# A delta-rule attention and two MLPs in one kernel: another written-out order for the first layer, and the last output tile shared by two engines

## The chip, the cores and the metric

One core of one Trainium2 chip runs the whole program. The metric is the device time of one execution in microseconds (us), as the median of several runs. A profile is one more execution, recorded by the hardware profiler; times inside it count from its first instruction.

## What is computed

Three stages follow each other, all in fp32 on the outside:

```python
# attention, per batch and head, over 768 steps t (head_dim 48)
k_n = k / (norm(k) + 1e-6)
y[t]  = q[t] @ state
state = state + beta[t] * outer(k_n[t], v[t] - state.T @ k_n[t])
# first layer: 3072 tokens, 384 -> 2048 -> 384
h = maximum(x @ w_in, 0); x = (h * h) @ w_out
# second layer: 3072 tokens, 384 -> 1536 -> 384
out = (sigmoid(x @ w_gate) * (x @ w_val)) @ w_out2
```

The weights come in as 64-bit words that hold doubles; the kernel turns them into fp32 itself.

## The kernel before, in words

**Precision.** A product with the weights is made of three: each operand is kept as a high and a low part (`xhi`, `xlo`; `w1h` and what is loaded as `il`; `gh`, `gl`), and hi*hi, lo*hi and hi*lo are added up in PSUM. The attention's products are plain fp32, and the trace shows each of them as two matmuls.

**Attention.** The 768 steps are cut in chunks of 64; two chunks (`st` 0 and 1) form a group `g`, 0 to 5. For each chunk small matmuls (16 to 64 rows and columns) make the scores (`scores_a`, L346; `scores_p`, L364), the inverse of a triangular matrix (rows on VectorE, `row16` L439 and `row` L448; the joins L483 to L521 for group 0 and 1; `n_piece` L523, `w_piece` L538), what the old state gives (`ks_piece`, L550), the new rows (`t_piece`, L571), the new state (`s_piece`, L582) and the output (`y_piece`, L600). Chunk after chunk hangs on the state of the one before. `y_rows` (L619) moves an output by DMA from `yt` to `xr`, where features lie along partitions; in group 0 three of its seven DMAs are issued by ScalarE, all others by SyncE. `x_split` (L638) makes `xhi` on ScalarE and `xlo` on VectorE.

**First layer.** `moe1_h` (L677) makes one of 16 blocks of 128 hidden units for the 512 tokens of a group: 9 matmuls of 128x512, then three passes on ScalarE (`relu2`, L681). `moe1_g` (L692) makes `gl` on VectorE, `moe1_o` (L701) adds the block to the output with 9 more matmuls. Numbers run through: `h,17` is group 1, block 1. The low parts of the weights are read back from DRAM into rings of three buffers each (`fetch_low`, L648).

**Conversion of the first layer's weights.** For each block f: fetch (`f`), two ScalarE passes (`hi`, L151), a shift on VectorE (`b`, L157), an addition on VectorE (`b2`, L160), the high part on ScalarE (`ch`, `parts` L201), the low part on GpSimd (`cl`, `rests` L207), and its store (`sl`, `keep` L211). The three steps `hi`, `b`, `b2` stand in both programs alike. The second layer's weights go through the same (`w2,i,k`).

**What sets the order.** `ORDER` (L41) is a list of 921 tokens such as `h,17` or `ks,0,1` (names in the table `fns`, L747; a token's numbers are group and chunk, or block). The loop at L766 runs them one after the other, and every engine and DMA queue executes what it gets strictly in that order, waiting by semaphores for what others make. `d,n` are n spare matmuls. The list ends with `h,80` and `h,81`; the rest of the first layer (L942) and the whole second layer are emitted by loops with plans of their own.

**The end.** The last group's output is made in four tiles `m` of 36 matmuls each (L1169 to L1191). Tile 0 and 2 are copied out of PSUM by ScalarE, 1 and 3 by VectorE; SyncE stores each in two DMAs.

Of the kernel before, what the change touches and what calls it, by code (L numbers as in the profile page):

```python
# [46 lines left out]
b2,5 a,1,1 ti,1 sl,3 y,0,0 r,1,0 s,0,0 r,1,1 cl,4 f,6 f,7 r,1,2 sl,4 z,0,0 hi,6 ks,0,1 d,1 b,6 b2,6 d,1 ch,5
cl,5 x,0,0 kc,1,1 t,0,1 hi,7 y,0,1 r,1,3 r,1,4 d,1 d,2 to,1 b,7 p,1,1 f,8 sl,5 q,1,0 v,1,0 z,0,1 b2,7 ch,6 cl,6
x,0,1 ja,1,1 hi,8 p,1,0 h,0 ja,1,0 ch,7 kn,2,0 b,8 li,2 h,2 t1,1 g,0 li,1 b2,8 h,1 sl,6 g,2 li,3 lw,3 g,1 sv,1,0
cl,7 lw,0 ch,8 o,0 f,9 lw,2 s,0,1 hi,9 b,9 sl,7 jb,1,1 f,10 h,3 b2,9 ks,1,0 lw,1 kt,2,1 cl,8 n,1,1 hi,10 g,3  # L50
sq,2,0 sl,8 b,10 ch,9 li,7 sm,3,0 o,1 cl,9 jb,1,0 f,11 b2,10 h,7 sm,2,0 o,2 hi,11 b,11 b2,11 jc,1,0 li,4 kn,2,1
sl,9 ch,10 sq,2,1 lw,4 n,1,0 sm,2,1 jc,1,1 no,2 h,4 cl,10 f,12 hi,12 a,2,1 g,4 ch,11 li,5 o,3 b,12 sl,10 g,7 h,5
lw,5 a,2,0 b2,12 w,1,0 o,4 cl,11 f,13 hi,13 b,13 g,5 li,6 lw,6 b2,13 li,8 w,1,1 lw,7 ti,2 t,1,0 k2,1,0 h,6 y,1,0
r,2,0 v,1,1 o,5 g,6 ch,12 s,1,0 sl,11 kz,2,0 r,2,1 h,8 f,14 sv,1,1 ks,1,1 li,9 o,6 cl,12 sl,12 li,10 hi,14 b,14
ch,13 cl,13 g,8 b2,14 li,11 lw,8 o,7 h,9 g,9 r,2,2 r,2,3 t,1,1 z,1,0 x,1,0 h,11 o,8 lw,9 h,10 sl,13 ch,14 f,15
hi,15 g,11 b,15 g,10 b2,15 y,1,1 o,9 li,12 h,12 g,12 lw,11 p,2,0 li,13 lw,10 r,2,4 r,2,5 cl,14 lw,12 o,10 ch,15
sl,14 z,1,1 li,14 h,13 x,1,1 o,11 g,13 h,14 g,14 lw,13 li,16 o,12 h,16 r,2,6 lw,14 cl,15 sl,15 k2,1,1 v,2,0 o,13
o,14 li,15 h,15 r,2,7 li,18 g,16 lw,15 g,15 h,18 s,1,1 kz,2,1 o,15 g,18 r,2,8 li,17 h,17 g,17 lw,16 li,21 r,2,9
lw,18 sv,2,0 o,16 li,19 kn,3,1 h,19 lw,17 r,2,10 to,2 o,17 g,19 w2,0,0 o,18 t1,2 sq,3,1 h,21 li,20 sm,3,1 w2,0,1
p,2,1 lw,20 no,3 n,2,0 lw,19 o,19 h,20 q,2,0 kc,2,0 ks,2,0 w,2,0 g,20 lw,25 kt,3,1 w2,0,2 v,2,1 li,24 h,24 n,2,1  # L60
a,3,1 g,24 o,20 sv,2,1 w2,0,3 q,2,1 g,21 kt,3,0 li,23 a,3,0 li,22 h,22 g,22 w,2,1 ti,3 r,3,0 li,25 t,2,0 lw,21
o,21 k2,2,0 r,3,1 r,3,2 lw,22 o,22 po,0 h,23 g,23 ks,0,0 lw,23 y,2,0 h,25 o,23 r,3,3 r,3,4 li,26 h,26 kc,2,1
li,28 g,25 lw,24 o,24 kz,3,0 s,2,0 z,2,0 x,2,0 r,3,5 o,25 li,27 h,27 g,26 g,27 k2,2,1 lw,26 ks,2,1 v,3,1 kn,4,1
h,28 li,29 g,28 r,3,6 o,26 h,29 lw,27 t,2,1 o,27 li,31 w2,1,0 w2,1,1 y,2,1 li,30 r,3,7 h,30 lw,29 kn,5,0 sq,5,0
sq,4,1 g,29 r,3,8 lw,28 o,28 p,3,0 sm,4,1 h,31 w2,0,4 lw,30 li,32 li,34 z,2,1 lw,33 li,33 r,3,9 x,2,1 o,29 g,30
s,2,1 w2,1,2 h,32 o,30 g,31 h,34 w2,1,3 r,3,10 g,32 to,3 lw,31 o,31 kz,3,1 v,3,0 sv,3,0 h,33 p,3,1 g,33 kn,4,0
t1,3 n,3,0 li,35 lw,32 o,32 kc,3,0 g,34 sq,4,0 sm,4,0 no,4 o,33 li,37 w2,1,4 ks,3,0 li,36 n,3,1 kt,4,0 h,35
w2,2,0 w2,2,1 lw,34 h,36 w,3,0 g,35 a,4,0 o,34 lw,37 w2,2,2 li,38 kt,4,1 g,36 a,4,1 w,3,1 ti,4 lw,35 r,4,0 h,37
li,40 o,35 lw,36 h,40 po,1 g,37 r,4,1 r,4,2 o,36 t,3,0 r,4,3 o,37 r,4,4 h,38 kz,4,0 li,41 sv,3,1 g,38 q,3,0
w2,2,3 y,3,0 li,39 h,39 lw,38 o,38 lw,40 g,39 p,4,0 kc,3,1 g,40 r,4,5 li,43 lw,39 o,39 k2,3,0 s,3,0 r,4,6 h,43  # L70
z,3,0 h,41 o,40 g,41 ks,3,1 x,3,0 g,43 v,4,0 kc,4,0 li,42 li,44 lw,41 h,42 g,42 r,4,7 li,46 o,41 r,4,8 w2,2,4
t,3,1 r,4,9 r,4,10 q,3,1 h,44 y,3,1 w2,3,0 lw,42 o,42 g,44 li,45 w2,3,1 w2,3,2 lw,43 w2,3,3 o,43 kz,4,1 h,45
z,3,1 lw,44 p,4,1 g,45 x,3,1 li,47 h,46 o,44 lw,45 h,47 g,47 o,45 li,48 lw,52 li,49 lw,46 h,49 g,46 k2,3,1
w2,3,4 to,4 t1,4 lw,47 o,46 w2,4,0 h,48 g,49 w2,4,1 g,48 s,3,1 li,50 w2,4,2 li,52 n,4,0 sv,4,0 o,47 kn,5,1
w2,4,3 h,52 g,52 n,4,1 ks,4,0 kt,5,0 lw,48 o,48 sq,5,1 sm,5,1 sm,5,0 no,5 li,53 lw,49 h,50 w,4,1 li,51 kt,5,1
a,5,1 lw,50 v,4,1 o,49 w2,4,4 w2,5,0 sv,4,1 lw,51 h,51 w,4,0 w2,5,1 g,50 a,5,0 g,51 li,55 o,50 ti,5 h,53 w2,5,2
w2,5,3 o,51 q,4,0 t,4,0 lw,53 r,5,0 r,5,1 g,53 li,54 h,54 o,52 po,2 r,5,2 r,5,3 h,55 g,54 g,55 o,53 lw,54 y,4,0
w2,5,4 w2,6,0 w2,6,1 o,54 li,56 h,56 r,5,4 k2,4,0 w2,6,2 w2,6,3 li,57 lw,56 g,56 lw,55 s,4,0 h,57 g,57 kc,4,1
o,55 o,56 li,58 r,5,5 q,4,1 ks,4,1 lw,57 li,59 h,58 z,4,0 o,57 r,5,6 g,58 t,4,1 r,5,7 li,60 h,60 li,61 x,4,0
w2,6,4 lw,58 h,59 w2,7,0 g,59 o,58 lw,59 g,60 lw,60 li,62 lw,61 y,4,1 w2,7,1 k2,4,1 o,59 z,4,1 w2,7,2 w2,7,3  # L80
li,63 h,61 x,4,1 g,61 h,62 li,67 g,62 li,64 r,5,8 r,5,9 lw,62 o,60 h,63 lw,63 o,61 r,5,10 w2,8,0 h,64 li,66 g,64
g,63 s,4,1 to,5 w2,8,1 o,62 li,65 h,65 v,5,0 o,63 lw,66 w2,7,4 h,66 g,65 g,66 t1,5 lw,64 o,64 li,68 h,67 k2,5,0
g,67 w2,8,2 lw,65 q,5,0 kc,5,0 lw,68 w2,8,3 sv,5,0 o,65 o,66 h,68 lw,67 ks,5,0 n,5,0 li,69 kz,5,0 li,72 w2,9,0
h,69 g,68 o,67 w2,9,1 o,68 p,5,0 w,5,0 li,70 h,70 g,69 lw,69 w2,8,4 g,70 lw,70 h,72 lw,71 w2,9,2 o,69 li,71
li,74 w2,9,3 po,3 t,5,0 h,71 g,71 o,70 n,5,1 y,5,0 li,73 h,73 g,73 lw,72 w2,9,4 g,72 o,71 w2,10,0 lw,73 w2,10,1
li,76 w2,10,2 h,74 o,72 v,5,1 sv,5,1 o,73 g,74 li,77 h,76 g,76 w,5,1 s,5,0 li,75 h,75 z,5,0 lw,75 g,75 lw,74
# [1189 lines left out]
```

## Time and profile before

| | us |
|---|---|
| three timed runs | 1047.8, 1048.55, 1052.04 |
| median | 1048.55 |
| the profiled execution, its own time | 1056.13 |
| its span, first to last instruction | 1054.4 |
| TensorE busy in the span | 990.7 (94%) |
| mean granted TensorE clock | 0.991 |
| VectorE, ScalarE, GpSimd busy | 665.0, 502.6, 170.7 |
| DMA queue "instruction", q8 | 91 packets, 1.49 MB |

PE is TensorE's matmuls, PEld its weight loads, DVE VectorE, ACT ScalarE, POOL GpSimd, SP SyncE. A wait named "issue" is one in which the engine waited for nothing that the profile shows. A row of the timeline gives start, duration, engine, line, operation, out<-in, shape and count, and in brackets the idle time just before with what ended it.

### The profile page before, as it was taken

The numbers are of one execution on the slowest core, as the hardware profiler recorded it, in microseconds if no ns is written. First come the engines' busy times: TensorE is split into PE (matmuls) and PEld (weight loads), VectorE is DVE, ScalarE is ACT, GpSimd is POOL, SyncE is SP. The second block draws the span as 40 slices with busy tenths as digits, with TensorE's granted clock in tenths as the row PEclk, the third lists the DMA queues.
The fourth block names the chain that finished last, engine by engine and source line by source line (L and its number), as shares of the span: only waits on it lengthen the run. The fifth ranks groups of instructions, "written<-read, shape, count | busy, mean of one in ns | idle before, by whom it ended". The sixth has DMA issues, their size and how long they took to land. (4 is left out here: it accounts for less than half of the span.)

```text
span 1054.4 us, 27329 instructions
## 1 busy us (share of the span) xinstructions
PE 990.7 (94%) x11609; PEld 819.3 (78%) x11611; DVE 665.0 (63%) x1338; ACT 502.6 (48%) x827; POOL 170.7 (16%) x141
## 2 busy tenths in 40 slices
...
GB/s 259 204 167 165 215 219 189 207 200 129 203 211 194 192 202 216 179 189 203 175 188 215 239 227 235 234 259 128 213 173 140 104 127 97 91 134 165 121 2 59
DMA packets 84394, 186.31 MB, mean 177 GB/s; under 512 B 22320, under 2 KB 57520, under 8 KB 79664
## 3 DMA queue, kind: packets, MB, share of 16 engines
...
q8 instruction: 91, 1.49, 0.6%
...
HBM read 139.30 MB, written 40.50 MB: 171 GB/s over the span
## 5 line engine op out<-in xcount | busy, mean ns | idle before, releaser
L695 DVE TENSOR_TENSOR gl<-gg,gh 128x512 fp32r<-128x512 f32 x96 | 65.6, 688 | 106.5 <-ACT gg L689 106.4
L686 ACT ACTIVATE gg<-h 128x512 f32<-128x512 f32 x96 | 57.4, 598 | 143.7 <-PE h L672 140.6
L710 PE MATMUL o<-gh,il 128*128 128x512 f32 x288 | 113.8, 395 | 0.0
L997 PE MATMUL o<-gh,wo 128*128 128x512 f32 x270 | 91.7, 390 | 0.0
L710 PE MATMUL o<-gh,w1h 128*128 128x512 f32 x216 | 88.0, 407 | 0.0
L710 PE MATMUL o<-gl,w1h 128*128 128x512 f32 x216 | 85.7, 397 | 0.3 <-DVE gl L695 0.3
L672 PE MATMUL h<-xhi,il 128*128 128x512 f32 x288 | 82.0, 393 | 1.1 <-DMA il<-w1d 1.1
L1116 PE MATMUL gy<-xa,wg 128*128 128x512 f32 x288 | 75.5, 391 | 2.2 <-DVE gateC L1030 1.9
L1116 PE MATMUL gx<-xa,wg 128*128 128x512 f32 x288 | 75.5, 391 | 0.0
L303 POOL TENSOR_TENSOR v<-v,br 128x768 f32<-128x768 f32 x12 | 19.5, 1631 | 314.1 <-DMA v<-in_vn_dram 193.0
L1116 PEld LDWEIGHTS gy<-xa,wg 128*128 128x128 f32 x288 | 53.8, 188 | 14.6 <-DVE gateC L1030 3.0
L672 PE MATMUL h<-xhi,w1h 128*128 128x512 f32 x216 | 64.4, 407 | 0.4 <-ACT xhi L126 0.4
L672 PEld LDWEIGHTS h<-xhi,il 128*128 128x128 f32 x288 | 54.5, 189 | 13.2 <-DMA il<-w1d 1.5
L1116 PEld LDWEIGHTS gx<-xa,wg 128*128 128x128 f32 x288 | 53.9, 188 | 12.3 <-DVE valC L1030 0.7
L710 PEld LDWEIGHTS o<-gh,il 128*128 128x128 f32 x288 | 54.9, 191 | 10.7
L688 ACT ACTIVATE gh<-gg 128x512 fp32r<-128x512 f32 x96 | 60.7, 632 | 3.1
L689 ACT ACTIVATE gg<-gg 128x512 f32<-128x512 f32 x96 | 60.7, 632 | 3.1
L672 PE MATMUL h<-xlo,w1h 128*128 128x512 f32 x216 | 61.2, 392 | 0.0
L997 PEld LDWEIGHTS o<-gh,wo 128*128 128x128 f32 x270 | 50.7, 188 | 10.6
L997 PE MATMUL o<-gl,wo 128*128 128x512 f32 x135 | 52.6, 390 | 0.0
L462 DVE TENSOR_TENSOR tt<-tt,tmp 128x40 f32<-128x40 f32 (+7 forms) x208 | 49.2, 269 | 1.4
L850 POOL TENSOR_TENSOR wg<-wr,wg 128x640 fp32r<-128x640 f32 (+1 forms) x20 | 30.9, 1552 | 116.1 <-ACT wg L845 116.1
(221 smaller groups left out, 2173.6 us busy)
## 6 DMA issues: line engine op xcount, KB each, us to landing
...
```

Source lines behind the costliest of these rows:

```text
L303: nc.gpsimd.tensor_tensor(out=v, in0=v, in1=br[:, 16 * st:16 * st + 16].unsqueeze(2).to_broadcast([128, 16, HD]), op=ALU.mult)
L462: nc.vector.tensor_tensor(out=tt[:, 0:j, lo:hi], in0=tt[:, 0:j, lo:hi], in1=tv[i], op=ALU.subtract)
L672: nc.tensor.matmul(out=ps[:, cs], lhsT=w[:, kc * 128:kc * 128 + 128], rhs=x[:, kc, cs], start=(i == 0 and kc == 0), stop=(i == 2 and kc == ...
L686: nc.scalar.activation(out=gg, in_=ps, func=ACTF.Relu)
L688: nc.scalar.activation(out=gh, in_=gg, func=ACTF.Square)
L689: nc.scalar.activation(out=gg, in_=gg, func=ACTF.Square)
L695: nc.vector.tensor_tensor(out=gl, in0=gg, in1=gh.bitcast(F32), op=ALU.subtract)
L710: nc.tensor.matmul(out=po[m], lhsT=w[:, cs], rhs=x, start=(f == 0 and i == 0), stop=(f == NF1 - 1 and i == 2),)
L850: (eng or nc.vector).tensor_tensor(out=t, in0=raw_w[q][:, a:b], in1=h.bitcast(F32), op=ALU.subtract)
L997: nc.tensor.matmul(out=po2[g, m], lhsT=w, rhs=x, start=start, stop=stop)
L1116: nc.tensor.matmul(out=ps, lhsT=a, rhs=c, start=k == 0 and u == us[0], stop=k == 2 and u == us[-1],)
```

## The change

The list is replaced from its second line on. It is a permutation: the same 921 tokens, so the same instructions on every engine apart from the end. The last tile (`m == 3`) is copied half by VectorE and half by ScalarE, and the second of its two stores is issued by ScalarE.

```diff
 ORDER = """
 d,1 kn,0,0 sq,0,0 kn,0,1 sm,0,0 kt,0,0 sq,0,1 be sm,0,1 no,0 kt,0,1 d,1 a,0,0 cj kn,1,1 q,0,1 kc,0,1 f,0 a,0,1
...
-b,1 b2,1 sq,1,1 k2,0,0 f,2 cl,0 sq,1,0 hi,2 ja,0,1 b,2 kc,0,0 q,0,0 p,0,0 sm,1,1 v,0,0 kt,1,0 sl,0 ch,1 jb,0,1
...
+sm,1,0 b,3 k2,0,0 jc,0,0 q,0,0 ch,2 no,1 jb,0,1 f,4 p,0,0 b2,3 n,0,0 sl,1 sv,0,0 kt,1,0 cl,2 w,0,0 f,5 sl,2 ch,3
+cl,3 hi,4 a,1,0 t,0,0 v,0,1 b,4 hi,5 b2,4 ch,4 li,0 sv,0,1 b,5 b2,5 f,6 d,1 s,0,0 n,0,1 a,1,1 sl,3 jc,0,1 q,1,1
...
-            if m % 2:
+            if m == 3:
+                nc.vector.tensor_copy(out=o_out[:, :, 0:2], in_=o_in[:, :, 0:2])
+                nc.scalar.copy(out=o_out[:, :, 2:4], in_=o_in[:, :, 2:4])
+            elif m % 2:
                 nc.vector.tensor_copy(out=o_out, in_=o_in)
...
-                nc.sync.dma_start(out=out[r0:r0 + C, :], in_=ob[64 * b:64 * b + 64])
+                (nc.scalar if m == 3 and b else nc.sync).dma_start(out=out[r0:r0 + C, :], in_=ob[64 * b:64 * b + 64])
```

Three places show how instructions move. First TensorE, from `t,0,0` (L575, the first chunk's new rows) to `t,0,1` (the second's), before and then in the changed program. L529 is `n,0,1`, L544 `w,0,1`, L352 `a,1,1`, L516 `jc,0,1`, L611 `y,0,0`, L588 `s,0,0`, L557 `ks,0,1`.

```order
20 L575 MATMUL att<-v,t_111 64x48 x32
21 L529 MATMUL att<-t_111,am 32x32 x32
22 L544 MATMUL att<-n,xi 32x32 x32
23 L352 MATMUL att<-kt 64x64 x32
24 L611 MATMUL att<-pm,u_116 64x64 x32
25 L588 MATMUL att<-u_116,k_118 64x48 x32
26 L557 MATMUL att<-state,kc 64x48 x32
```

```order
22 L575 MATMUL att<-v,t_111 64x48 x32
23 L745 LDWEIGHTS join
24 L745 MATMUL idle<-join 128x512
25 L588 MATMUL att<-u_116,k_118 64x48 x32
26 L529 MATMUL att<-t_111,am 32x32 x32
27 L352 MATMUL att<-kt 64x64 x32
28 L516 MATMUL att<-xi,join 32x16 x32
29 L557 MATMUL att<-state,kc 64x48 x32
30 L544 MATMUL att<-n,xi 32x32 x32
31 L611 MATMUL att<-pm,u_116 64x64 x32
32 L575 MATMUL att<-v,t_111 64x48 x32
```

The state `s,0,0` moves from behind four other pieces to right behind `t,0,0`; the output `y,0,0` moves back behind `ks,0,1` and `w,0,1`, and `jc,0,1`, which stood ahead of `t,0,0`, now follows it.

Second ScalarE, from the copy of the first chunk's output (L616) to that of the second. `xr` rows are DMAs that ScalarE issues for `z,0,0`; L130 and L133 are `hi`, L205 is `ch`, L126 the split of the first chunk's output, L580 the copy that follows `t,0,1`. Before, and then in the changed program:

```order
45 L631 DMA xr<-yt 32x512
46 L634 DMA xr<-yt 48x256
47 L635 DMA xr<-yt 16x256
48 L130 ACTIVATE wt<-w1s_1171 128x768
49 L133 ACTIVATE w1s_1171<-w1s_1171 128x768
50 L205 CAST w1h_98<-wt 128x768
51 L126 CAST xhi<-xr 128x3x256
52 L580 COPY u_117<-att 128x8x48 x2
53 L130 ACTIVATE wt<-w1s_1173 128x768
54 L133 ACTIVATE w1s_1173<-w1s_1173 128x768
55 L616 COPY yt<-att 128x512 x2
```

```order
48 L616 COPY yt<-att 128x512 x2
49 L631 DMA xr<-yt 32x512
50 L634 DMA xr<-yt 48x256
51 L635 DMA xr<-yt 16x256
52 L580 COPY u_117<-att 128x8x48 x2
53 L126 CAST xhi<-xr 128x3x256
54 L205 CAST w1h_99<-wt 128x768
55 L616 COPY yt<-att 128x512 x2
```

The two conversions between the copies are gone from here, and the split L126 stands behind the copy L580 of the second chunk instead of ahead of it.

Third SyncE's queue around `z,4,1`, late in the first layer; `il` rows are loads of low parts into the two rings, L284 is `q,4,1`, L222 and L147 belong to `w2`. Before, and then in the changed program:

```order
236 L147 DMA raw<-in_w_dram 128x1536
237 L650 DMA il<-w1d 128x384 x4
238 L298 DMA k_119<-in_ks_dram 128x768
239 L629 DMA xr<-yt 48x512
240 L630 DMA xr<-yt 48x512
```

```order
238 L222 DMA w2d<-y 128x768
239 L147 DMA raw<-in_w_dram 128x1536
240 L650 DMA il<-w1d 128x384 x5
241 L629 DMA xr<-yt 48x512
242 L630 DMA xr<-yt 48x512
```

Five ring loads instead of four stand between the fetch L147 and `z,4,1`; the last of the five is `lw,62`. On TensorE the first matmuls that need that output, `h,64`, follow after `h,63`, `o,61` and `o,62`.

## Rows read from the trace of the kernel before

**Rows 1.** The page: busy us and instructions by engine; the code queue

```profile
PE 990.7 (94%) x11609; PEld 819.3 (78%) x11611; DVE 665.0 (63%) x1338; ACT 502.6 (48%) x827; POOL 170.7 (16%) x141
...
q8 instruction: 91, 1.49, 0.6%
```

**Rows 2.** Windows: stretch, length, busy (count) of PE, PEld, DVE, ACT, POOL, clock, DMA

```profile
25.00:50.00 25.00, 9.88 (x537) 9.10 (x537) 14.44 (x24) 9.47 (x15) 3.63 (x2) 1.00 0.79 226
50.00:75.00 25.00, 18.51 (x617) 17.34 (x618) 7.68 (x14) 17.39 (x29) 7.52 (x6) 1.00 0.52 171
75.00:100.00 25.00, 17.79 (x605) 15.48 (x602) 22.15 (x45) 11.84 (x19) 5.73 (x3) 1.00 0.51 144
100.03:106.85 6.82, 6.40 (x61) 5.27 (x57) 3.82 (x6) 2.85 (x4) 1.47 (x1) 0.50 0.54 176
236.56:243.39 6.83, 6.11 (x73) 4.67 (x74) 2.76 (x4) 1.23 (x2) 0.00 (x0) 0.50 0.15 46
```

**Rows 3.** Waits of PE from 0 to 103 us: total, times, longest

```profile
PE att L490 <- issue: 6.1, 2, 4.9
...
PE att L387 <- issue: 3.9, 1, 3.9
...
PE att L575 <- issue: 2.9, 2, 2.3
PE att L502 <- issue: 2.8, 1, 2.8
```

**Rows 4.** Timeline of PE, pieces of the front and the first layer's first product

```profile
43.01 2.40 PE L387 MATMUL att<-q,kc 48*64 48x64 f32 x40 [3.85 <-issue]
...
57.81 2.00 PE L544 MATMUL att<-n,xi 32*32 32x32 f32 x64
...
93.07 0.35 PE L613 MATMUL att<-q,state 48*64 48x64 f32 x8
...
103.09 1.65 PE L672 MATMUL h<-xhi,w1h 128*128 128x512 f32 x3 [0.42 <-ACT xhi L126]
```

**Rows 5.** Timeline of ACT, copies of the front (columns as in rows 4)

```profile
67.03 0.86 ACT L580 COPY u<-att 128x384 f32<-128x384 f32 x2 [2.87 <-PE att L575]
...
77.94 1.07 ACT L616 COPY yt<-att 128x512 f32<-128x512 f32 x2 [0.20 <-PE att L611]
...
82.04 2.06 ACTq L635 DMA_DIRECT2D xr<-yt  x1
...
87.52 0.83 ACT L126 CAST xhi<-xr 128x768 fp32r<-128x768 f32 x1 [0.84 <-DMA kc<-in_kq_dram]
...
93.48 1.07 ACT L616 COPY yt<-att 128x512 f32<-128x512 f32 x2 [1.56 <-PE att L613]
```

**Rows 6.** Timeline of PE, two waits and a product later in the first layer

```profile
121.88 0.78 PE L557 MATMUL att<-state,kc 48*64 48x48 f32 x35 [1.96 <-issue]
...
226.23 0.84 PE L672 MATMUL h<-xhi,il 128*128 128x512 f32 x3
226.91 0.84 PE L672 MATMUL h<-xlo,w1h 128*128 128x512 f32 x3
...
237.28 0.37 PE L352 MATMUL att<-kt 48*64 48x64 f32 x1 [2.53 <-issue]
```

**Rows 7.** The tile xr: ns min/median/max, first and last start

```profile
L635 SPq DMA_DIRECT2D xr<-yt x22: 519/590/1574, 80.5 to 552.3; - x22
...
DMA to landing us min/median/max: 1.8/2.4/5.6
```

**Rows 8.** The end: lines 1183, 1185 and 1191, columns as in rows 7

```profile
L1183 DVE COPY obt<-r x2: 558/558/558, 1037.5 to 1050.0; 128x384 f32<-128x384 f32 x2
...
L1185 ACT COPY obt<-r x2: 480/481/482, 1031.3 to 1043.8; 128x384 f32<-128x384 f32 x2
...
DMA to landing us min/median/max: 2.1/2.2/2.2
```

More of the change, by code (lines that the diff above doesn't have):

```diff
@@ L42 @@
 d,1 kn,0,0 sq,0,0 kn,0,1 sm,0,0 kt,0,0 sq,0,1 be sm,0,1 no,0 kt,0,1 d,1 a,0,0 cj kn,1,1 q,0,1 kc,0,1 f,0 a,0,1
-kn,1,0 k2,0,1 cs ti,0 kt,1,1 r,0,0 r,0,1 r,0,2 r,0,3 r,0,4 f,1 to,0 hi,0 b,0 b2,0 p,0,1 ja,0,0 t1,0 ch,0 hi,1
-b,1 b2,1 sq,1,1 k2,0,0 f,2 cl,0 sq,1,0 hi,2 ja,0,1 b,2 kc,0,0 q,0,0 p,0,0 sm,1,1 v,0,0 kt,1,0 sl,0 ch,1 jb,0,1
-sm,1,0 b2,2 cl,1 no,1 f,3 hi,3 b,3 jb,0,0 jc,0,0 f,4 sl,1 b2,3 ch,2 cl,2 li,0 sv,0,0 n,0,0 kc,1,0 hi,4 a,1,0
-v,0,1 kn,3,0 sv,0,1 sl,2 ch,3 w,0,0 sq,3,0 jc,0,1 b,4 cl,3 t,0,0 f,5 hi,5 b2,4 q,1,1 n,0,1 w,0,1 ch,4 kt,2,0 b,5
@@ L47 @@
[L47 to L86, printed above, removed]
@@ L87 @@
-o,74 kc,5,1 ks,5,1 x,5,0 q,5,1 lw,78 h,77 w2,10,3 lw,76 li,78 o,75 g,77 kz,5,1 k2,5,1 t,5,1 h,78 p,5,1 o,76
-lw,77 y,5,1 g,78 li,81 li,79 w2,10,4 lw,79 h,79 g,79 w2,11,0 o,77 z,5,1 x,5,1 lw,81 o,78 o,79 w2,11,1 w2,11,2
-lw,82 li,82 h,81 lw,80 g,81 li,80 w2,11,3 h,80 g,80 po,4 li,83
+kn,1,0 k2,0,1 cs ti,0 kt,1,1 r,0,0 r,0,1 r,0,2 r,0,3 r,0,4 f,1 to,0 sq,1,1 hi,0 d,1 b,0 b2,0 ch,0 v,0,0 p,0,1
+ja,0,0 t1,0 hi,1 cl,0 b,1 f,2 ja,0,1 b2,1 sq,1,0 hi,2 kc,0,0 sm,1,1 f,3 ch,1 sl,0 jb,0,0 b,2 b2,2 cl,1 hi,3
@@ new lines @@
+sm,1,0 b,3 k2,0,0 jc,0,0 q,0,0 ch,2 no,1 jb,0,1 f,4 p,0,0 b2,3 n,0,0 sl,1 sv,0,0 kt,1,0 cl,2 w,0,0 f,5 sl,2 ch,3
+cl,3 hi,4 a,1,0 t,0,0 v,0,1 b,4 hi,5 b2,4 ch,4 li,0 sv,0,1 b,5 b2,5 f,6 d,1 s,0,0 n,0,1 a,1,1 sl,3 jc,0,1 q,1,1
+kn,3,0 ch,5 ks,0,1 sq,3,0 cl,4 hi,6 w,0,1 b,6 ti,1 f,7 v,1,0 r,1,0 r,1,1 r,1,2 sl,4 b2,6 f,8 y,0,0 r,1,3 kc,1,1
+z,0,0 t,0,1 x,0,0 ch,6 r,1,4 to,1 y,0,1 d,1 d,2 cl,5 sl,5 q,1,0 kc,1,0 p,1,1 sm,3,0 z,0,1 x,0,1 ja,1,1 cl,6
+p,1,0 hi,7 hi,8 li,2 li,1 h,2 b,7 b2,7 sl,6 ch,7 lw,4 g,2 ja,1,0 h,0 kn,2,1 h,1 t1,1 b,8 g,0 s,0,1 lw,0 g,1
@@ new lines @@
+sv,1,0 f,9 cl,7 hi,9 b,9 b2,8 lw,1 jb,1,1 li,5 sl,7 ch,8 o,0 n,1,1 b2,9 ch,9 cl,8 sq,2,1 li,4 ks,1,0 o,1 li,3
+f,10 hi,10 kn,2,0 b,10 h,3 b2,10 lw,3 g,3 jb,1,0 sm,2,1 sq,2,0 lw,2 sl,8 ch,10 o,2 o,3 sm,2,0 no,2 f,11 n,1,0
+kt,2,0 cl,9 hi,11 jc,1,0 h,4 w,1,0 a,2,0 sl,9 cl,10 f,12 b,11 b2,11 h,5 g,4 ch,11 hi,12 li,7 g,5 b,12 h,7 kt,2,1
+lw,6 li,6 o,4 sl,10 jc,1,1 lw,8 b2,12 a,2,1 h,6 g,6 lw,5 cl,11 f,13 o,5 hi,13 t,1,0 b,13 w,1,1 k2,1,0 o,6 sl,11
+b2,13 ti,2 li,8 li,9 lw,7 ch,12 cl,12 h,8 ch,13 f,14 y,1,0 g,7 li,10 g,8 r,2,0 o,7 r,2,1 hi,14 b,14 v,1,1 sl,12
@@ new lines @@
+h,9 b2,14 s,1,0 z,1,0 h,10 r,2,2 li,11 sv,1,1 ks,1,1 cl,13 g,10 ch,14 o,8 li,12 g,9 h,12 t,1,1 r,2,3 x,1,0 lw,9
+g,12 sl,13 o,9 f,15 hi,15 b,15 b2,15 ch,15 h,11 g,11 lw,10 cl,14 li,13 lw,11 o,10 r,2,4 h,13 g,13 r,2,5 sl,14
+cl,15 kz,2,0 lw,12 y,1,1 o,11 lw,13 sl,15 z,1,1 x,1,1 o,12 o,13 p,2,0 li,14 h,14 r,2,6 li,15 g,14 h,15 g,15
+li,16 v,2,0 h,16 lw,14 o,14 lw,15 r,2,7 r,2,8 o,15 li,19 h,19 g,16 r,2,9 li,18 k2,1,1 s,1,1 lw,16 li,17 h,17
+o,16 lw,17 g,17 h,18 kn,4,0 kz,2,1 p,2,1 kn,3,1 o,17 g,18 r,2,10 kc,2,0 sq,3,1 to,2 li,21 sv,2,0 h,21 ks,2,0
@@ new lines @@
+lw,18 n,2,1 o,18 g,19 li,22 sm,3,1 no,3 lw,19 t1,2 o,19 h,22 g,21 kt,3,1 n,2,0 li,20 a,3,1 kt,3,0 h,20 a,3,0
+w,2,0 g,20 w2,0,0 lw,20 w2,0,1 li,23 w,2,1 ti,3 w2,0,2 lw,21 lw,23 g,22 w2,0,3 po,0 o,20 o,21 h,23 li,24 t,2,0
+h,24 q,2,0 r,3,0 lw,22 r,3,1 r,3,2 y,2,0 g,23 o,22 li,25 g,24 lw,24 r,3,3 r,3,4 r,3,5 h,25 o,23 o,24 kc,2,1
+k2,2,0 v,2,1 g,25 z,2,0 lw,26 s,2,0 li,28 li,26 r,3,6 lw,28 lw,25 w2,1,0 h,26 sv,2,1 h,28 o,25 g,26 ks,2,1 li,27
+ks,0,0 h,27 o,26 li,29 q,2,1 lw,27 g,27 r,3,7 t,2,1 g,28 kn,4,1 h,29 li,32 sq,4,1 x,2,0 o,27 li,30 kc,3,1 h,30
```

25 lines of the change are left out of this document (added).

## The prediction

> **What bounds the kernel.** I read the page first: TensorE is busy for 990.7 of 1054.4 us [rows 1], so only the rest can be won by an order. The windows then show where that rest lies: of 25 us each, TensorE works 9.88, 18.51 and 17.79 between 25 and 100 us, and from then on nearly all the time but for short waits [rows 2, 6]. The front ends when the first product of the first layer starts, at 103.09, released by ScalarE's `xhi` [rows 4]. Everything that the list can give must make this start earlier, or take away one of the later waits.
>
> The front has two limits. One is the chain of attention pieces and copies. The other is in the waits: of TensorE's idle time before 103 us, 6.1, 3.9, 2.9 and 2.8 us end with "issue" [rows 3], in the middle of runs of equal matmuls, where no data are missing. The queue named instruction moved 1.49 MB in 91 packets, 16.4 KB each; TensorE's 11609 matmuls and 11611 loads are 255 for each packet [rows 1]. So I read these waits as TensorE waiting for its code, a packet at a time: 128 small matmuls with their loads. At the counts of the windows 128 matmuls took 25 x 128/537 = 6.0 us, then 5.2 and 5.3 us [rows 2], though their own work is about 4 us (64 take 2.0 us [rows 4]). The Trainium skill, page "Runtime: NRT & Kernel Launch", section "Instruction fetch mechanics", has the same blocks, 16 KiB for 256 instructions, the next fetched while one executes, and calls the cost of crossing "mostly hidden". The trace agrees on the size; it differs on the hiding, with 15.7 us of such waits [rows 3]. By that rule the front would go by its chain.
>
> **The front, by the chain alone.** The two programs hold the same instructions before the first `h`, so the stops on code come after the same counts. Up to the stop that ends at 43.01 [rows 4] nothing that matters moves: the matmuls before it are the same but for 24 of `p,0,0` that become 24 of `jb,0,0`. From 43.0 the new order is the rest of `jb,0,0` (1.5 us, by its share of a piece), then `jc,0,0`, `jb,0,1`, `n,0,0`, `w,0,0`, `a,1,0` and `t,0,0`, six pieces at 2.0 us [rows 4], `p,0,0` at 3.8 (64 at the pace of 40 in 2.40 [rows 4]) and two copies between `n`, `w` and `t` that nothing covers, 1.2 us each, which is near the longest copy in the group [rows 5]. That is 19.7 us: `t,0,0` ends at 62.7, its copy of 0.86 at 63.6, where the trace of before has 67.9 [rows 5]; `jc,0,1`, which stood ahead of it, is now behind.
>
> Then `s,0,0` follows at once: 65.6. Behind it `n,0,1`, `a,1,1`, `jc,0,1` and `ks,0,1` take 8 us, 73.6; VectorE's four passes on `ks` are covered by `w,0,1` and `y,0,0`, 77.6; `t,0,1` ends at 79.6. ScalarE first copies `y,0,0` (1.07, to 78.7), issues three DMAs, then copies `t,0,1`, until about 82. `y,0,1` takes two pieces, 86. Here the new ScalarE order costs something: the copy of `y,0,1` stands behind `xhi` of the first chunk, and that waits for `z,0,0`. Before, the last of these DMAs was issued at 82.04 and `xhi` began at 87.52, 8.5 us after the copy of `y,0,0` ended [rows 5]; 1.6 us of it ScalarE spent on state copies, which now lie earlier, so I take 6.9. With `xhi` (0.83), a `ch` of the same length and the copy (1.07), the copy of `y,0,1` ends at 78.7 + 6.9 + 2.7 = 88.3, if TensorE has `y,0,1` by then, as it has. Before it ended at 94.55, and the first `h` came 8.5 us later [rows 4, 5]. So the chain alone gives a gain of 6.2 us, less about 1 for banks of PSUM, of which the front has three: **-5**.
>
> **The front, paced by code.** From 43.0 to the end of `y,0,0` the new order holds 1064 matmuls, 8.3 packets. At 5.2 us each that is 86.2, with its copy 87.3, and the chain from there gives 87.3 + 6.9 + 2.7 = 96.9 instead of 94.55: **+2.3**. The reason is that `y,0,0` stands later now, while all of the second chunk's conversions wait less. The break-even is a copy of `y,0,0` that ends at 85.0, thus 4.9 us a packet. Nothing in the rows says which pace the new mix of loads and matmuls gets; I take the middle of -5 and +2.3, **-1.3**.
>
> **Later waits.** TensorE stops on code for 1.96 us at 119.9 and for 2.53 at 234.8 [rows 6], and the granted clock is 0.50 (1.2 GHz) for 6.82 us around the first product and for 6.83 us after the second wait [rows 2], which costs half of such a stretch, 3.4 us. Small pieces stand about as densely in the new list at these places, so I take **0**, and as ends -4.5 (both waits gone) and +3.4 (one more stretch at half clock).
>
> **A new wait at `h,64`.** SyncE now has `lw,62` ahead of `z,4,1`, and that load needs the buffer that `o,60` frees. From there seven DMAs of some 0.57 us each, 1.8 us to the last landing [rows 7] and `xhi` of 0.83 [rows 5] make 6.6 us; TensorE has `h,63`, `o,61` and `o,62` meanwhile, 27 matmuls at 0.68/3 us [rows 6], 6.1 us. With the queue's own delay **+0.8**, between 0 and 1.5.
>
> **The rest of the permutation.** GpSimd is busy for under 8 us of each window; VectorE has room before 75 us, 14.44 and 7.68, and is full after it, 22.15 of 25 [rows 2], with the rows of group 1, most of which now stand behind the passes on `ks`. The first product needs the same conversions, up to block 2; those that were moved (`hi`, `b`, `b2` of blocks 7 and 8 behind the second split) cost nothing while ScalarE idles there. If that cover goes, the three ScalarE passes of the first `h` start up to 1.8 us later, with two more `h` to work on meanwhile.
>
> **The end.** After the last matmul a copy of 0.56 us [rows 8] and two stores, one issue of some 0.5 us behind the other, 2.1 us to landing [rows 8]. Half a copy on each of two engines is not in the trace; between nothing and half of 0.56 I take 0.2 saved, and one issue, 0.5: **-0.7**. ScalarE's queue is the unknown: in the front its DMA took up to 5.6 us [rows 7], under load. That would make the end 2.7 us later; with an idle queue, like SyncE's 2.1, nothing. I take the idle one, which is nearest: the store is alone there.
>
> **Sum.** -1.3 + 0 + 0.8 - 0.7 = -1.2 us. It is made on an execution of 1056.13 us, 0.7% above the median of 1048.55; carried over as a difference it gives 1047.3.
>
> **Rivals.** *The code is always there*: the new order spreads small pieces and loads so that no packet is late. Then the chain decides, -5, the two later waits go, -4.5, and 0.8 - 0.7 remain: -9.4, 1039.2 us. It decides from a pace below 4.9 us on. For it: the packets' pace was 6.0 us under the heaviest DMA load (share 0.79) and 5.2 at 0.52 [rows 2], so lighter loads help. Against it: the load before 100 us is the same bytes, only sooner. Chance 0.30. The rule of the Trainium skill, "Runtime: NRT & Kernel Launch", would come out here too.
>
> *The split blocks ScalarE*: with the pace at 5.2 us, the copy of `y,0,1` waits behind `xhi`, +2.3; TensorE, thinly used between 87 and 103, then gets one more stretch at half clock, +3.4; with +0.8 and -0.7 that is +5.8, 1054.3 us, slower. It decides as soon as the copy of `y,0,0` ends after 85.0. For it: all three windows have a pace above 5.0 [rows 2]. Against it: the stretch at half clock around the first product is already there. Chance 0.20.
>
> That the change doesn't do what its words say can be excluded in part: the three conversion steps are the same in both programs, only their places differ.
>
> **Numbers.** My forecast, 1047.3, has the chance 0.50, and with the bounds of its terms 1043 to 1051 as its own range. About 0.5% (5.2 us) is what a measurement of this kernel can tell from no change: 1043.3 and 1053.8. The forecast with its range lies within; 0.02 of it falls below, and of the two rivals nearly all falls outside. So faster 0.32, same 0.48, slower 0.20. The range takes in the centres of both rivals, 1039.2 to 1054.3, and leaves out their outer halves.
>
> **What would show it.** Start of the first `h`: 98 by the chain, 102 as forecast, 105 if ScalarE is blocked. "Issue" waits of TensorE before it: 16 us again, or a few. The copy of `y,0,0` before or after 85.0, and what ScalarE waits for ahead of its second copy. A wait for `xhi` of about 1 us near 455. The last store landing 2.6 us after the last matmul instead of 3.3. I am wrong if the first `h` stays within 2 us of 103 and the time still moves by more than 5: then something later in the first layer counts that I set to 0.

## The result, and the profile after

The changed program takes 1064.59 us (1061.99 to 1068.79, 4 runs), the one before 1049.63 on the same chip (1047.8 to 1052.04, 4 runs): 1.0145 times the time, between 1.0102 and 1.0188. It is slower by 1.5%, outside the range. The profiled executions lie closer together than that, 1061.99 against 1056.13 us, since that of before is a long one of its kind and that of after a short one; so what follows rests on the runs with an interval, and on profiles for the places.

The page of after, to be read against [rows 1]: TensorE has the same instructions, but for a record, and 4.8 us more busy time, and the code queue moved the same 91 packets.

```profile
PE 995.5 (94%) x11608; PEld 821.8 (78%) x11611; DVE 673.9 (64%) x1338; ACT 503.2 (47%) x828; POOL 170.9 (16%) x141
...
q8 instruction: 91, 1.49, 0.6%
```

The front, first TensorE's waits from 0 to 103 us (as [rows 3]), then its timeline, then ScalarE's:

```profile
PE att L490 <- DVE t L472: 15.6, 2, 10.9
...
PE att L516 <- issue: 5.1, 1, 5.1
...
PE att L502 <- issue: 4.5, 2, 2.4
```

```profile
95.53 1.26 PE L490 MATMUL att<-t,am 32*16 32x16 f32 x128 [4.73 <-DVE t L472]
96.73 3.70 PE L387 MATMUL att<-q,kc 48*64 48x64 f32 x64
100.36 0.79 PE L672 MATMUL h<-xhi,w1h 128*128 128x512 f32 x1
```

```profile
79.47 1.07 ACT L616 COPY yt<-att 128x512 f32<-128x512 f32 x2 [1.19 <-PE att L611]
...
95.92 0.83 ACT L126 CAST xhi<-xr 128x768 fp32r<-128x768 f32 x1 [7.50 <-DMA xr<-yt]
```

The first `h` starts at 100.36 instead of 103.09 [rows 4]. So the front is not where the time went. TensorE's waits from 103 to 630 us, which is the rest of the first layer, of the kernel before and then of after:

```profile
PE att L352 <- issue: 2.5, 1, 2.5
PE att L557 <- issue: 2.0, 1, 2.0
PE att L557 <- ACT gh L688: 1.7, 1, 1.7
PE h L672 <- DMA il<-w1d: 1.1, 1, 1.1
```

```profile
PE att L529 <- issue: 2.0, 1, 2.0
PE h L672 <- ACT xhi L126: 1.6, 2, 1.4
PE h L672 <- DMA il<-w1d: 1.5, 2, 1.2
PE att L613 <- issue: 1.5, 1, 1.5
PE h L672 <- issue: 1.4, 1, 1.4
PE att L544 <- issue: 1.3, 1, 1.3
PE att L557 <- ACT gh L688: 1.3, 1, 1.3
PE att L352 <- issue: 1.0, 1, 1.0
```

Two stops on "issue" have become five, and waits for other engines and for low parts of the weights are spread over the layer. Just behind the wait of `ks,1,1` (L557), from 171.0 us, and from 239.3 us, within the stop of L544 that ends at 239.6, the granted clock is 0.50, its lower level of 1.2 GHz (windows as in [rows 2]):

```profile
171.00:174.41 3.41, 3.40 (x36) 2.83 (x37) 3.13 (x8) 0.32 (x1) 0.99 (x1) 0.50 0.97 368
239.27:246.09 6.82, 6.49 (x21) 5.08 (x22) 5.74 (x12) 3.74 (x6) 0.00 (x0) 0.50 0.19 57
```

From the first `h` to the end of the last `o` the layer takes 528.6 us instead of 519.6; what follows it takes 431.3 and 431.7. In these two profiles, which are 5.9 us apart, the whole loss is inside the first layer.

The end, on VectorE, ScalarE and the two queues; the last four landings took 2.1 to 2.4 us:

```profile
1056.22 0.36 DVE L1183 COPY obt<-r 128x192 f32<-128x192 f32 x1 [11.93 <-PE r L1176]
1056.61 0.32 ACT L1184 COPY obt<-r 128x192 f32<-128x192 f32 x1 [6.15 <-DVE obt L1183]
1056.96 0.47 SPq L1194 DMA_DIRECT2D out_dram<-obt  x1
1056.96 0.55 ACTq L1194 DMA_DIRECT2D out_dram<-obt  x1
```

The two halves are not copied side by side: ScalarE waits for VectorE, because the program gives its copy a wait for VectorE's semaphore. Two halves take 0.71 us where one whole copy took 0.56 [rows 8]; what is saved is the second issue.

### The profile page after: what moved, and what is told of

It is laid out like the page before. It is cut to its first block, busy times and chain, and to the rows that moved or that the text cites. A ratio compares the mean times of both kernels' runs of the same rounds, so it can differ in the third digit from the quotient of the medians.

```text
span 1060.3 us, 27331 instructions
## 1 busy us (share of the span) xinstructions
PE 995.5 (94%) x11608; PEld 821.8 (78%) x11611; DVE 673.9 (64%) x1338; ACT 503.2 (47%) x828; POOL 170.9 (16%) x141
## 4 chain that ended last, share of the span: by engine, by line
PE 73%; DVE 3%; issue 3%; DMA 2%; POOL 1%; ACT 1%; SPq 1%; ACTq 0%; DVEq 0%; POOLq 0%
PE o L710 17%; PE h L672 16%; PE gx L1116 11%; PE gy L1116 11%; PE o L997 10%; PE r L1176 2%; PE att L611 1%; PE att L557 1%; PE att L575 1%; PE att L544 1%; DVE wr L837 1%; PE att L613 1%; DMA w2d<-y 1%; PE att L372 1%; PE att L529 1%
## 5 line engine op out<-in xcount | busy, mean ns | idle before, releaser
L695 DVE TENSOR_TENSOR gl<-gg,gh 128x512 fp32r<-128x512 f32 x96 | 69.2, 725 | 115.6 <-ACT gg L689 115.5
L455 DVE TENSOR_TENSOR tmp<-xi,tt 128x40 f32<-128x40 f32 (+7 forms) x208 | 51.6, 282 | 1.2
```

Source lines behind the costliest of these rows:

```text
L455: nc.vector.tensor_tensor(out=tv[i], in0=xi[:, 0:j, j].unsqueeze(2).to_broadcast([128, j, n]), in1=tt[:, j, lo:hi].unsqueeze(1).to_broadca ...
L695: nc.vector.tensor_tensor(out=gl, in0=gg, in1=gh.bitcast(F32), op=ALU.subtract)
```

## The experiments

All ratios are to the kernel before, run on the same chip; 1.011 is 11.5 us. "Old" and "new" are the two lists. Where nothing is said of the end, it is the old one.

### Which part of the change: list or end, front or rest

list_only has the new list with the old end, tail_only the old list with the new end. newfront and newrest cut the list at `p,1,0`, just ahead of the first `h`:

```diff
-ORDER = old
+ORDER = new up to p,1,0, then what is left in the old order     (newfront)
+ORDER = old up to p,1,0, then what is left in the new order     (newrest)
```

> The new list with the old end. Both theories (the later part of the new list loses, or its front does) put the whole loss into the list: ratio 1.012 to 1.017 to the program before, as the changed program. If the shared last tile were the loser, the ratio would fall to 1.000 to 1.004.

> The old list with the new end. The two halves of the last copy ran one after the other in the changed program's trace (0.36 and 0.32 us), so the last landing comes 3.15 us after the last matmul instead of 3.34: ratio 0.999 to 1.001. Rival (the shared end loses): 1.008 or more.

> New list up to p,1,0, the last attention piece ahead of the first h; all tokens left then in the old list's order. Theory A (the front gains, the later order loses): first h at 99 to 101 us and the gain kept, ratio 0.993 to 0.998. Theory B (the new front leaves debts, conversions not yet done and a half clock, that the rest pays): ratio 1.006 to 1.015 although the first h is early.

> Old list up to p,1,0, the rest in the new list's order. Theory A (the later order loses): first h at 102 to 104 us and ratio 1.014 to 1.020, more than the change itself because the gain of the front is missing. Theory B (the front's debts): ratio 0.998 to 1.004.

Measured: list_only 1.011 (1.0069 to 1.0152), tail_only 0.9979 (0.9954 to 1.0004), newfront 0.9993 (0.9963 to 1.0024), newrest 1.0104 (1.0066 to 1.0142). The order behind `p,1,0` carries the loss, the front and the end change next to nothing. In the eight profiles with the new front in this and the next two sections and the result, the first `h` starts at 101.6 on average (100.2 to 104.0), in the six with the old front at 102.5 (101.3 to 103.3).

### Single spots mended: nothing won

The new list has places that look like causes. Around 168 us VectorE gets the shift and addition of block 14 ahead of the three additions to the state (L598), and `ks,1,1` waits for them:

```profile
167.69 0.55 DVE L136 TENSOR_SCALAR wt<-wt 128x768 uint32<-128x768 uint32 x1
...
168.36 0.96 DVE L140 CUSTOM_DVE_ANT_0 wt<-wt,raw 128x1536 uint16<-128x1536 uint16 x1
...
169.24 1.72 DVE L598 TENSOR_TENSOR state<-state,att 128x384 f32<-128x384 f32 x3
...
169.93 0.81 PE L557 MATMUL att<-state,kc 48*64 48x48 f32 x34 [1.29 <-ACT gh L688]
```

(The row names ScalarE's `gh`, long done; what is late is the state.) The edits, each from the new list, and the last one the first of them put into the old list:

```diff
-r,2,1 hi,14 b,14 v,1,1 sl,12 h,9 b2,14 s,1,0 z,1,0 h,10 r,2,2 li,11 sv,1,1 ks,1,1 cl,13
+hi,14 v,1,1 sl,12 h,9 s,1,0 z,1,0 h,10 r,2,1 r,2,2 li,11 sv,1,1 ks,1,1 b,14 b2,14 cl,13       (rep_s, rep_all)
-w,2,0 g,20 w2,0,0 lw,20 w2,0,1 li,23 w,2,1 ... o,20 o,21
+w,2,0 g,20 lw,20 o,20 w2,0,0 w2,0,1 li,23 w,2,1 ... o,21       (rep_w, rep_all)
-w2,7,3 li,63 li,64 lw,62 h,63 o,61 o,62 z,4,1
+w2,7,3 z,4,1 li,63 li,64 lw,62 h,63 o,61 o,62       (rep_all)
-n,5,1 y,5,0 li,82 sv,5,1 o,72
+n,5,1 li,82 sv,5,1 o,72 y,5,0       (rep_all)
-s,1,0 sl,11 kz,2,0 r,2,1 h,8 f,14 sv,1,1 ks,1,1
+f,14 hi,14 r,2,1 b,14 b2,14 s,1,0 sl,11 kz,2,0 h,8 sv,1,1 ks,1,1       (def_s, in the old list)
```

> The new list with the old end (1064.8 us alone, 1.011 of the kernel before); three pieces of the list are moved: b,14 and b2,14 (VectorE's sum and square of block 14) behind ks,1,1, and r,2,1 behind s,1,0. Theory one, the loss is in single spots, each with its own late releaser: VectorE's three additions to the state start when s,1,0's matmuls end, as in the old list, the wait of ks,1,1 (1.45 us) goes, and the 3.41 us at half clock right behind it (1.7 us) go too: 3 us less, about 1061.7, ratio 1.008. Theory two, the new list bunches small matmuls everywhere and pays for it in code and clock wherever the next bunch lies: the wait at ks,1,1 may go, but the time stays within 1 us of 1064.8.

> The new list with the old end; only lw,20 and o,20 are moved, to stand between w,2,0 and w,2,1, which the new list has back to back on TensorE (128 matmuls of 64 x 64 in one row). Theory one: the stop of 1.3 to 1.5 us in the middle of w,2,1 at about 240 us, which waits for no semaphore, goes, and with it the half clock behind it (3.4 to 6.8 us at half speed, 1.7 to 3.4 us lost): 3 to 4.5 us less, 1060.5 to 1062, ratio 1.007. Theory two: the stop only moves to the next small matmuls, and the time stays within 1 us of 1064.8.

> The new list with the old end and four spots mended: the two of the runs before, z,4,1 four pieces earlier (so that x,4,1 has its rows before h,64), and y,5,0 behind o,72 instead of next to n,5,1. Theory one: 3 + 3.5 + 1 + 1.6 us, 9 us less in sum: 1056, ratio 1.003, and the time lost between the first h and the end of the first layer is within 3 us of the old list's. Theory two: 1062 to 1066, with new stops at other places.

> The kernel before (1051.9 us) with one spot made as in the new list: f,14, hi,14, r,2,1, b,14 and b2,14 stand ahead of s,1,0, so that VectorE has them before the three additions to the state, and ks,1,1 follows. Theory one: a wait of 1 to 1.5 us at ks,1,1 and half clock behind it, 2 to 4 us more, ratio 1.002 to 1.004. Theory two: at this place the old list has enough between s and ks to hide it, ratio 1.000, no wait over 0.5 us at ks,1,1.

Measured: rep_s 1.0115 (1.0076 to 1.0154), rep_w 1.0101 (1.0058 to 1.0144), rep_all 1.0114 (1.0067 to 1.016), def_s 1.0015 (0.999 to 1.0041). The spots react: in rep_s the wait of `ks,1,1` is gone and with it the half clock behind it, in def_s `ks,1,1` waits 3.4 us, against 1.7 in the profile of before and none in tail_only (in def_s and before this wait ends where a code block does, see below, so part of it may be code). But the time does not follow. The 9 us that rep_all was to win (1.003) lie outside its interval; the 3 to 4.5 us of rep_s and rep_w are too small to be told by theirs. In rep_s the waits for low parts grew from 1.3 us to 2.6; in rep_w other stops took the place of the one removed; in rep_all `h,63` waits 2.8 us for its low half, because I had moved the seven DMAs of `z,4,1` ahead of that load.

### Which stretch

early_new is new up to and with `o,30` (about 297 us) and old from there, late_new the reverse; from_o8 is old up to `o,8` (about 170 us), then new. rep_more mends seven spots of the new list:

```diff
-n,1,1 b2,9 ch,9 cl,8 sq,2,1 li,4 ks,1,0 o,1
+n,1,1 o,1 b2,9 ch,9 cl,8 sq,2,1 li,4 ks,1,0
-z,1,1 x,1,1 o,12 o,13 p,2,0 li,14 h,14
+li,14 z,1,1 x,1,1 o,12 o,13 p,2,0 h,14
-z,2,0 lw,26 s,2,0 li,28 li,26
+li,26 z,2,0 lw,26 s,2,0 li,28
-h,64 v,5,0 r,5,6 h,65 g,64 o,63
+o,63 h,64 v,5,0 r,5,6 h,65 g,64
...
```

> The new list up to and with o,30 (about 297 us), then the pieces that are left in the old list's order; old end. If the loss is made up of single spots spread over the first layer, it halves: by the curves of time lost in earlier runs the new order has lost some 5 us more than the old by o,30, so about 1057, ratio 1.005. If it comes from the stretch behind o,30 alone, 1052, ratio 1.000; if from before it alone, 1064, ratio 1.011.

> The old list up to and with o,30, then the pieces that are left in the new list's order; old end. The other half of the same question: by the same curves the new order loses another 5 us between o,30 and the end of the layer, at the waits of 1 to 2 us near 390, 471 and 525 us: 1057, ratio 1.005. If the waits behind o,30 hang on what the new list did before it (buffers and queues running late), 1052, ratio 1.000.

> The new list with the old end and seven spots mended: b,14 and b2,14 behind g,10 and r,2,1 behind s,1,0; o,20 between w,2,0 and w,2,1; y,5,0 behind o,72; li,14 ahead of z,1,1; li,26 ahead of z,2,0; o,63 ahead of h,64; o,1 between n,1,1 and ks,1,0. If the loss is the sum of these spots and a mended spot does not open another: 2 (near 118 us) + 3 + 1.3 + 3 + 1.3 + 1 + 1.7, 13 us less than 1064.8: 1052, ratio 1.000 to 1.003. If each wait that is taken away only uncovers the next (a code packet, or SP's queue, that TensorE then reaches too early): 1060 or more, ratio over 1.007.

> The old list up to and with o,8 (about 170 us), then the pieces that are left in the new list's order; old end. Known are 1.0104 for the cut ahead of the first product and 1.0026 for the cut at o,30 (297 us). The stretch up to o,8 holds the wait at ks,1,1 with its half clock and the denser pieces of blocks 9 to 14. If this stretch carries most, 1.003 to 1.005; if the stretch from 170 to 297 us carries most (the two w pieces side by side, the late low halves of h,14 and h,26), 1.007 to 1.010.

Measured: early_new 1.0151 (1.0106 to 1.0196), late_new 1.0026 (0.9996 to 1.0056), from_o8 1.0059 (1.0033 to 1.0085), rep_more 1.0122 (1.0082 to 1.0163). With the cut moved from 103 to 170 to 297 us the loss falls from 1.0104 to 1.0059 to 1.0026: it has no single place (though each cut also moves code borders, which the next section is about). early_new says less than it seems, since at its seam alone `h,34` waits 5.2 us for a low half that is loaded late there. And with seven spots mended rep_more, which was to win 13 us, still has 11.4 us of stops on "issue", one of 4.6 us where the new list had 1.0 to 1.5. Mending moved the stops elsewhere.

### The place of the code blocks

That led back to the prediction's own reading of the front: TensorE's code comes in packets of 256 instructions. If every stop without a releaser is such a border, it lies at a fixed count. I numbered TensorE's loads and matmuls in the traces of all the kernels here and took, for each stop over 0.8 us, the number of the row that ends it, modulo 256. Of two old and two new orders (time : remainder; some of the front's are left out):

```
before     36.6:187  43.0:185  51.2:184  65.7:179  98.9:171  121.9:169  237.3:152
phase_old  35.3:186  42.0:183  64.7:177  99.9:169 119.8:169  141.2:168  165.6:162  241.5:153  372.4:126  527.3:102
after      32.6:186  43.7:185  48.5:185 106.4:166 117.9:164  139.1:160  239.6:141  525.9:99
three_new  33.2:187  43.2:186  48.6:186  76.0:175 117.8:166  134.8:165
```

Of 180 such stops in 20 profiles 179 lie on this one line, which falls slowly from 187 to 99; the other is one of 0.9 us at 60.0 us in phase_old. The line falls because the rows leave out TensorE's semaphore instructions: with those that the traces keep counted in, the 179 stand at remainders of 190 to 195, and there are as many borders as code packets, 91, or 92 in block_old and three_new. A packet shows with them: at the 17 stops of before, after, phase_old, block_old and three_new behind 103 us, one packet of the code queue is moved, and the stop ends 1.2 to 1.6 us after it. Taken in order, one packet to one border, this holds in all 20 profiles: the 179 stops end 1.1 to 1.8 us after the end of their packet, and at the other 1623 borders TensorE comes to the row of remainder 195 later than 1.1 us after the packet's end, 5.9 us after it in the median. So a stop is a border that TensorE reaches before its packet is in. In after, the queue in the window from 523.0 to 524.5 us, and TensorE, which stops inside a run of 8 equal matmuls of `y,5,0`:

```profile
q8 instruction: 1, 0.02, 5.2%
```

```profile
524.09 0.28 PE L613 MATMUL att<-q,state 48*64 48x64 f32 x5
525.87 0.33 PE L613 MATMUL att<-q,state 48*64 48x64 f32 x3 [1.50 <-issue]
```

If so, the same list must change its time when all borders are moved, with no piece moved. 64 spare matmuls with their loads, in the first microseconds where TensorE waits for data, move them by half a block:

```diff
+    def spare(n):
+        for _ in range(n):
+            nc.tensor.matmul(out=idle[0][:, 0:64], lhsT=zeros[:, 0:128], rhs=zeros[:, 0:64], start=True, stop=True)
...
-d,1 kn,0,0
+d,1 e,64 kn,0,0       (phase_old in the old list, phase_new in the new; e is spare)
```

> The kernel before with 64 spare matmuls of 64 columns (128 TensorE instructions with their loads, half a code block) in the first microseconds, where TensorE waits for its first data; their result is not used. If the old list owes its time to where its blocks of 256 instructions happen to fall, the stops that wait for no semaphore move and grow, and the time goes up by 5 us or more, towards 1060 (ratio 1.005 to 1.010). If the order itself matters and not the phase, ratio 1.000, between 0.997 and 1.003.

> The new list with the old end and the same 64 spare matmuls. If the new list only has an unlucky phase, it comes down to 1.003 to 1.006. If its order itself costs, 1.010 to 1.013 as without them, with the stops at other places.

Measured: phase_old 1.0146 (1.011 to 1.0182), phase_new 1.0143 (1.0109 to 1.0177). The old list, otherwise untouched, is as slow as the changed kernel. Its waits from 103 to 630 us, against two stops before:

```profile
PE att L502 <- issue: 3.2, 1, 3.2
PE att L611 <- issue: 2.7, 1, 2.7
PE h L672 <- issue: 2.5, 1, 2.5
PE att L588 <- issue: 2.3, 1, 2.3
PE o L710 <- ACT o L721: 1.9, 1, 1.9
PE att L352 <- issue: 1.8, 1, 1.8
PE att L613 <- issue: 1.4, 1, 1.4
```

Then the control, a shift by a whole block, and the two shifts of the new list that were left:

```diff
+e,64 behind the first d,1 and e,64 ahead of ja,0,0      (block_old, old list: 256 instructions)
+e,32 behind the first d,1                               (quarter_new, new list: 64)
+e,64 behind the first d,1 and e,32 ahead of ja,0,0      (three_new, new list: 192)
```

> The kernel before with twice 64 spare matmuls, 64 in the first microseconds and 64 in the wait before the first join at 20 us: 256 TensorE instructions with their loads, a whole code block, so that from then on the blocks begin at the same pieces as in the kernel before. If the place of the block boundaries is what cost phase_old its 1.0146: back at 1.000, between 0.997 and 1.003. If the spare matmuls themselves do it (by the clock, or by what they delay at the front): 1.015 as in phase_old, or more.

> The new list with the old end and 32 spare matmuls in the first microseconds: 64 instructions, a quarter of a block. If the new order is no worse than the old but for the place of its boundaries, one of the two phases not yet seen (a quarter, three quarters) comes near the kernel before: 1.000 to 1.004. If the order itself is worse (waits for ScalarE, VectorE and late low halves besides the code), both lie between 1.008 and 1.015.

> The new list with the old end and 96 spare matmuls, 64 in the first microseconds and 32 before the first join: 192 instructions, three quarters of a block. Same two readings as for a quarter: 1.000 to 1.004 at one of the two phases if only the boundaries' place is at fault, 1.008 to 1.015 at both if the order itself costs.

| list, shift in instructions | ratio | stops | at half clock | other waits | layer |
|---|---|---|---|---|---|
| old, 0 (before) | 1 | 4.5 | 14.0 | 3.5 | 519.6 |
| old, 0 (tail_only) | 0.9979 (0.9954 to 1.0004) | 4.6 | 6.4 | 1.1 | 514.3 |
| old, 256 (block_old) | 1.0008 (0.9976 to 1.0039) | 5.1 | 3.4 | 1.4 | 513.7 |
| old, 128 (phase_old) | 1.0146 (1.011 to 1.0182) | 14.3 | 24.4 | 3.5 | 534.1 |
| new, 0 (list_only) | 1.011 (1.0069 to 1.0152) | 7.5 | 15.4 | 3.8 | 526.6 |
| new, 64 (quarter_new) | 1.0102 (1.0067 to 1.0138) | 10.5 | 23.8 | 3.9 | 533.9 |
| new, 128 (phase_new) | 1.0143 (1.0109 to 1.0177) | 8.7 | 16.6 | 3.8 | 527.9 |
| new, 192 (three_new) | 1.0013 (0.9984 to 1.0043) | 5.1 | 16.5 | 3.8 | 523.7 |

The last four columns are us of one profile each, from the first `h` to the last `o`: TensorE's waits on "issue", the time at half clock, its other waits, the length. Half of the time at half clock is taken as lost, since there a product of 512 columns follows the one before after 0.43 us instead of 0.23 (`o` in after, at 173 and at 179 us). Stops, this half and other waits add up to 8 to 30 us, and the layer less that sum is 504 to 508 us in every row. That is where the time went. The spare matmuls cost nothing (block_old), half a block costs 1.5% in the old list, and at three quarters of a block the new list is as fast as the old one. The old list at a quarter and at three quarters was not tried.

The spare matmuls also change the clock, which is a rival for the 1.5%: in the profiles of phase_old, phase_new, block_old and three_new the granted clock is 0.50 for 78 to 89 us ahead of the first `h`, in the others for at most 8. It isn't the cause. block_old and three_new have it and lose nothing; and of phase_old's six executions three have it by their mean clock (0.947 to 0.952: 1065.3 to 1070.39 us) and three have not (0.987 to 0.990: 1061.06 to 1067.4 us), all of them far above 1052.68, the kernel before. Nor does the front take longer by it: the new list's matmuls between 30 and 90 us were busy for 42.58 us at 0.50 (three_new, 1459 of them) and for 43.50 us at 1.00 (quarter_new, 1510).

At three quarters of a block TensorE passes the place in `y,5,0` without a stop, eight matmuls in one row each time:

```profile
521.13 0.30 PE L613 MATMUL att<-q,state 48*64 48x64 f32 x8
521.25 0.30 PE L611 MATMUL att<-pm,u 64*64 64x64 f32 x8
521.37 0.30 PE L613 MATMUL att<-q,state 48*64 48x64 f32 x8
```

### A try at something faster

best is the old list with the new end and two pieces moved:

```diff
-n,1,1 hi,10 g,3 sq,2,0 sl,8 b,10 ch,9 li,7 sm,3,0 o,1
+hi,10 g,3 sq,2,0 sl,8 b,10 ch,9 li,7 sm,3,0 o,1 n,1,1
-li,82 h,81 lw,80 g,81 li,80
+li,80 li,82 h,81 lw,80 g,81
```

> The old list with the new end and two pieces moved: n,1,1 behind o,1, so that it no longer stands next to ks,1,0 (code stop of 1.1 to 2.0 us at 119 us and 3.4 us at half clock behind it), and li,80 ahead of li,82 (h,80 waits 0.65 to 1.4 us for it at 555 us). If both waits go and nothing takes their place: 2 + 1.5 + 1 + 2 us (the end), ratio 0.994 to 0.996. If a mended spot here too uncovers the next: 0.998, as with the new end alone.

Measured: 1.0017 (0.999 to 1.0044). The wait of `h,80` for its low half is gone; the stop at 119 us stayed, 2.5 us in `ks,1,0`, because moving `n,1,1` behind that border does not move the border, and stops of 1.5 and 1.7 us came at later ones. No version here beats the kernel before by more than its interval; the nearest is tail_only.

## Why the prediction was wrong

**The step that failed** is "Later waits": 0, with ends at -4.5 and +3.4, because "small pieces stand about as densely in the new list at these places". The order behind `p,1,0`, set at 0, measured 1.0104, some 11 us (newrest). Density was the wrong measure. The same list, equally dense everywhere, takes 1.0146 or 1.0008 times the time with its borders half a block or a whole one further on. A permutation leaves the total count alone, but between its first and last moved piece it shifts what stands at each border. I had used this for the front ("the stops on code come after the same counts") and did not follow the count past the first `h`. On the profiles, list_only has 3.0 us more stops than tail_only, 9.0 us more at half clock (4.5 lost) and 2.7 more of other waits, 10.2 of the 12.2 us by which its layer is longer.

**"The rest of the permutation": cost nothing.** Also wrong, by less. At all four shifts the new list has 3.8 to 3.9 us of waits for other engines and low parts, the old one at its own place 1.1 to 3.5: the state additions behind block 14's conversion (up to 1.5 us), `xhi` of `h,64` (0.7), the low half of `h,26` (up to 0.9). These are real, but at the right shift all that the new list costs is 1.0013 (0.9984 to 1.0043).

**The front**, -1.3: about right. `y,0,0` was copied by 80.54 (79.47 + 1.07), well before the break-even of 85.0, and the stops before 103 us fell from 17.0 to 12.0 (sums of all rows of that view). So the chain decided, as the first rival said, but it did not give its 5 us: the second chunk's rows landed at 95.9, and the join waited 4.73 us for VectorE's rows. The profile gives -2.7, the means over profiles -0.9, and newfront 0.9993. That the middle of two estimates came near is luck: the copy of `y,0,1` ended at 88.42, as the chain had it (88.3), but the first `h` came 11.9 us behind it and not 8.5, which takes back 3.4 us of the chain's gain.

**The wait at `h,64`**, +0.8 between 0 and 1.5: right in place and size. TensorE waits there for `xhi`:

```profile
472.64 0.96 PE L672 MATMUL h<-xhi,w1h 128*128 128x512 f32 x3 [1.38 <-ACT xhi L126]
```

In list_only it is 0.7 us, in late_new 1.2; in rep_all, with `z,4,1` ahead of the load, it is gone.

**The end**, -0.7: the sign was right in the profile, the size not. The issue was saved, the copy was not shared but done in two steps; from the end of the last matmul to the last landing it is 3.14 us instead of 3.34; tail_only's 0.9979 does not tell this from nothing. ScalarE's idle queue costs little, as assumed: its store landed after 2.37 us, SyncE's after 2.13.

**The rivals.** "The code is always there" has the mechanism, code, and the wrong sign; "the split blocks ScalarE" has the sign and the wrong place. What the text named as proof against itself happened nearly as written: the first `h` stayed within 3 us of 103, and the time moved by 15, by something later in the first layer.

**What stays open.** Why a packet is late at one border and not at the next is only read from the rows, not tried: at the five stops of after behind 103 us the packet starts 0.3 to 3.5 us after the block before it has begun and takes 0.9 to 1.3 us, and TensorE is through that block in 1.2 to 4.8 us; a block with products of 0.23 us each lasts up to 31 us, and behind 531 us no profile has a stop. That agrees with the Trainium skill, "Runtime: NRT & Kernel Launch", section "Instruction fetch mechanics", that the next block is fetched while one executes; that it is mostly hidden holds here for the large products only. Nor do the borders alone fix the stops: before and block_old have them at the same pieces, and both stop at `ks,1,0` (121.9 and 120.1 us), but the second stop is at 237.3 us in one and at 153.7 in the other. What makes the clock fall was not separated from the stops before it. And that the new list at three quarters of a block is no faster than the old one at 0, in spite of its earlier first `h`, I put down to its other waits without having tried it.
